# Row sums and causal convolution of the first batch on TensorE instead of DMA and GpSimd, in a fused attention, gated convolution and token-mixing kernel

## The chip, the cores and the metric

The kernel runs on one core of a Trainium2 chip. The metric is the device time of one execution in microseconds (us). TensorE (PE) multiplies and transposes, VectorE (DVE), ScalarE (ACT) and GpSimd (POOL) work elementwise, and SyncE (SP) issues all the transfers of this kernel. Each engine runs its own instructions in order and waits for the others by semaphores.

## The reference

Inputs are q, k, v of shape (4, 12, 448, 64) and seven weight matrices. Three parts follow one another:

```python
scores = where(upper triangle, -1e9, q @ k.T / 8)            # causal attention, 4 batches x 12 heads
attn = exp(scores - rowmax); attn = attn / (rowsum + 1e-9)
x = (attn @ v)                                               # (4, 448, 768)
gate_pre[s] = sum over t in 0..4 of conv_w[t] * x[s - 4 + t] # causal convolution, per channel
x = (sigmoid(gate_pre) * (x @ w_val)) @ w_out
theta = x @ w_theta
u = x + w_tok_r @ (x * cos(theta)) + w_tok_i @ (x * sin(theta))
out = u + max(u @ w_ch, 0)
```

## The kernel before

All activations lie transposed: channels on the 128 partitions, the 448 positions of a sequence along the free dimension. Heads are worked in pairs, so one pair (numbered g, 0 to 23; six to a batch) fills one block of 128 channels. A product that must be precise is split into fp32r parts: a high part, and a low part that is the rest, and three products of them are summed. Plain fp32 operands go to TensorE in the product of probabilities and v (`attn_AV`), and in all transposes.

The program is a list of attention steps, `attn_iter(i)` for each head i, with five segments each, and a list of dense steps, `dense(b)` for each batch. The attention of batch 0 and of the first heads of batch 1 is issued first, in 69 segments; then the dense steps of each batch run with the attention of the next one threaded between them. A scheduler may then move instructions within each engine's order.

A pair passes through these functions:

- `attn_T`: at the end of an odd head, q and k of the next pair are transposed, and `split_qk` copies them out of PSUM. ACT makes qs and kk, DVE makes the low parts of both; a second copy of kk is made by ACT where the table `K_DUP` has 2, and by POOL where it has 0.
- `attn_S`: scores in four chunks of 112 rows, two products each; DVE masks and takes the row maximum, ACT takes the exponential and its row sum.
- `attn_PT`: ten transposes of the probabilities, copied out of PSUM by ACT and DVE.
- `attn_R` and `attn_B`: the reciprocals of the row sums (tile rec, 112 x 8) are written to DRAM (tile rows) and read back, each row spread over 64 partitions, as the tile rb (128 x 448).
- `attn_AV`: sixteen TensorE instructions on two halves of the array, one for each head of the pair, into one PSUM tile.
- `attn_X1`: DVE multiplies that by rb into the tile xf (line 408); ACT and POOL split it into x_hi and x_lo.
- `attn_X2`: the convolution. For the first six pairs `CONV_POOL` has 1, and POOL does it: nine instructions of 128 x 448 (lines 423, 427, 430). ACT then takes tanh.
- `gemm_ahead`: six products of x_hi and x_lo with the first two column blocks of w_val, for the pairs of batch 0 alone (line 451).

Between these, DVE and ACT turn raw weights into fp32 (`to_f32`: lines 153, 156, 160 on DVE), and POOL splits the weights. The tiles in PSUM of the attention share six buffers.

The order in which a step stands comes from these lines:

```python
            if j == 1 and n == (X_LAST if g == NP else X_SEG):
                attn_X(g - 1)
```

so pair g - 1 is multiplied and convolved at the end of the odd head of pair g.

Of the kernel before, what the change touches and what calls it, by code (L numbers as in the profile page):

```python
# [14 lines left out]
ALU = mybir.AluOpType  # L15
# [6 lines left out]
ROUND = 12582912.0  # L22

X_SEG = 3
X_LAST = 3
U_DVE = (0, 1, 1, 1)
PT_DVE = (2, 2, 0, 0)
K_DUP = (2, 2, 2, 2, 2, 2, 0, 0, 0, 0, 0, 0, 0, 0, 0, 1, 0, 1, 0, 0, 0, 0, 0, 0)
X_LO = (0, 0, 0, 0, 0, 0, 0, 0, 0, 0, 0, 0, 0, 0, 1, 0, 0, 0, 0, 0, 0, 0, 0, 0)
H_LO = (1, 0, 1, 0)  # L30
O_LO = (0, 0, 0, 1)
# [18 lines left out]
def kernel(  # L50
# [49 lines left out]
    def psum(tag):  # L100
        at = "mm" if tag == "mm" else "at"
        return ps.tile([P, 512], F32, tag=at, name=f"ps_{tag}", bufs=2 if tag == "mm" else 6)
# [12 lines left out]
    def exp_set(*args, **kw):  # L115
        exps.append(nc.scalar.activation(*args, **kw))  # L116
# [131 lines left out]
    gates = {}  # L248
    rbs = {}
    row_at = {}  # L250
    ttr_ins = []
    hf_ins = []

# [115 lines left out]
    def attn_X(g):  # L369
        if not 0 <= g < B * NP:  # L370
            return
        attn_X1(g)
        attn_X2(g)

    def attn_R(g):
        if not 0 <= g < B * NP:
            return
        rec = pool.tile([CP, 2, NC], F32, tag="rec", name="rec")
        nc.vector.tensor_scalar(out=rec, in0=sums[g], scalar1=1.0e-9, scalar2=None, op0=ALU.add)
        nc.vector.reciprocal(rec, rec)  # L380
        rows = dram.tile([2, NC, CP], F32, tag="rows", name="rows", bufs=2)
        nc.sync.dma_start(out=rows.rearrange("h c p -> p h c"), in_=rec)
        row_at[g] = rows

    def attn_B(g):
        if g not in row_at:
# [30 lines left out]
    def attn_X2(g):  # L417
        b, hp = divmod(g, NP)
        x = xf[g % 2]
        gt = pool.tile([P, S], F32, tag="gate", name="gate", bufs=6)  # L420
        if CONV_POOL[g]:
            tp = pool.tile([P, S], F32, tag="tmp", name="tp")
            nc.gpsimd.tensor_scalar(
                out=gt, in0=x[:, 0:S], scalar1=cw[:, 0, hp : hp + 1], scalar2=1.0, op0=ALU.mult, op1=ALU.mult
            )
            for t in range(1, KW):
                nc.gpsimd.tensor_scalar(
                    out=tp, in0=x[:, t : t + S], scalar1=cw[:, t, hp : hp + 1], scalar2=1.0, op0=ALU.mult, op1=ALU.mult
                )
                nc.gpsimd.tensor_tensor(out=gt, in0=gt, in1=tp, op=ALU.add)  # L430
        else:
            nc.vector.tensor_scalar(out=gt, in0=x[:, 0:S], scalar1=cw[:, 0, hp : hp + 1], scalar2=None, op0=ALU.mult)
            for t in range(1, KW):
                nc.vector.scalar_tensor_tensor(  # L434
                    out=gt, in0=x[:, t : t + S], scalar=cw[:, t, hp : hp + 1], in1=gt, op0=ALU.mult, op1=ALU.add
                )
        exp_set(gt, gt, AF.Tanh, scale=0.5)
        gates[b, hp] = gt

    wn = [AHEAD]  # L440
# [172 lines left out]
    def attn_iter(i):  # L613
        g, j = divmod(i, 2)

        def seg(n):
            if j == 1 and n == (X_LAST if g == NP else X_SEG):
                attn_X(g - 1)

        attn_PT(i - 1, (0,))  # L620
        attn_S(i, 0)
# [16 lines left out]
        seg(3)  # L638
        yield
        if j == 0:  # L640
            attn_AV(g - 1)
            load_v(g + 1)
            attn_B(g - 1)
        if i == B * H:
            attn_X(g - 1)
        seg(4)
# [17 lines left out]
    for n in range(5 * (H + 1) + X_SEG + 1):  # L664
# [10 lines left out]
                        if m < AHEAD + 1:  # L675
                            split_w(m, g)
        i, c = divmod(n, 5)
        if AHEAD and i >= 4 and i % 2 == 0 and c == A_SEG and i // 2 - 2 < KC - 1:
            gemm_ahead(i // 2 - 2)
        if n == 5 * H - 3:  # L680
            with tc.issue_after(ttr_ins[-1].ins):
                for g in range(2):
                    load_w(AHEAD + 2, g)
    if AHEAD:
        gemm_ahead(KC - 1)
    for b in range(B):
        done = 0
        for y, _ in enumerate(dense(b)):
# [44 lines left out]
```

## Time and profile before

| | |
|---|---|
| median of 3 runs | 807.39 us (806.12 to 808.97) |
| profiled execution | 811.03 us, its span 809.2 us |
| TensorE busy | 725.1 us, 90% |
| VectorE, ScalarE, GpSimd busy | 493.8, 427.4, 316.2 us |
| mean granted TensorE clock | 0.949 of full speed |

The profile is of one execution. Busy time of TensorE counts an instruction from its start to its modelled end, whatever the clock; the granted clock is 1.0 at 2.4 GHz and 0.5 at 1.2 GHz. The work of the first batch's attention lies between 4 us and 124 us, where the first product of a dense step (line 472) begins. The rest of the span is dense steps with attention in between.

### The profile page before, as it was taken

What the parts mean: (1) busy time and instruction counts of PE and PEld (TensorE: products, weight loads), DVE (VectorE), ACT (ScalarE), POOL (GpSimd) and SP (SyncE); (2) the same over time, 40 slices, a digit from 0 to 9 for tenths busy, and PEclk for the clock granted to TensorE, in tenths of its full rate; (3) what the DMA queues carried; (4) which work ended last, traced back from release to release, by engine and by line L of the source; (5) the groups of instructions that cost most, each with busy time, mean ns of one, the idle gap of its engine ahead of it and who ended that gap; (6) DMA issues with size and microseconds to landing.
All of it is one profiled execution on the core that took longest, in us unless ns stands there. A gap on an engine that the chain in (4) does not pass through costs nothing.

```text
span 809.2 us, 11956 instructions
## 1 busy us (share of the span) xinstructions
PE 725.1 (90%) x3965; PEld 609.7 (75%) x3965; DVE 493.8 (61%) x1125; ACT 427.4 (53%) x998; POOL 316.2 (39%) x327
## 2 busy tenths in 40 slices
PE   5687889698598798999989899899999998999997
PEld 4455558577387686788978788788888787988996
DVE  4666869999999837535657645653666732114541
ACT  6767754465567744435687633444787622124401
POOL 0386976586355658123226610113234232201100
PEclk9888779789699999999999999999999999999999
DMA  9548627979576248778744259579824078774323
GB/s 233 125 104 182 151 47 200 236 238 294 142 221 140 63 133 225 225 234 184 157 136 86 60 144 190 148 221 196 178 58 102 12 140 215 214 212 139 98 57 90
DMA packets 151850, 126.01 MB, mean 156 GB/s; under 512 B 93519, under 2 KB 126829, under 8 KB 151789
## 3 DMA queue, kind: packets, MB, share of 16 engines
q1 hardware_dynamic: 151789, 125.25, 60.9%
q8 instruction: 31, 0.51, 0.3%
q14 instruction: 30, 0.25, 0.1%
HBM read 100.76 MB, written 24.47 MB: 155 GB/s over the span
## 4 chain that ended last, share of the span: by engine, by line
PE 54%; DVE 18%; DMA 9%; ACT 8%; POOL 6%; issue 4%; SPq 1%; ACTq 0%; POOLq 0%; DVEq 0%
PE ps_mm L472 28%; PE ps_mm L567 10%; PE ps_av L364 5%; PE ps_tr L341 3%; PE ps_s L320 2%; DVE gate L434 2%; PE ps_s L321 2%; DMA out_dram<-o 2%; DVE cv_raw L156 2%; DMA rb<-rows 2%; DMA scratch<-w_hl 2%; POOL gate L430 2%; DVE qs L111 1%; DMA rows<-rec 1%; ACT prob L116 1%
## 5 line engine op out<-in xcount | busy, mean ns | idle before, releaser
L472 PE MATMUL ps_mm<-act_hi,w_hl 128*128 128x448 f32 x864 | 274.1, 379 | 10.7 <-POOL w_hl L105 7.0
L472 PEld LDWEIGHTS ps_mm<-act_hi,w_hl 128*128 128x128 f32 x864 | 165.1, 193 | 27.9 <-POOL w_hl L105 9.4
L472 PE MATMUL ps_mm<-act_lo,w_hl 128*128 128x448 f32 x432 | 160.4, 373 | 0.0
L116 ACT ACTIVATE prob<-ps_s,negm 112x112 f32<-112x112 f32 x192 | 95.4, 498 | 71.4 <-DVE negm L322 69.4
L322 DVE CUSTOM_DVE_ANT_0 ps_s<-ps_s,mask 112x112 f32<-112x112 f32 x192 | 86.2, 454 | 76.3 <-PE ps_s L321 62.6
L320 PE MATMUL ps_s<-kk,qs 128*112 128x256 f32 x192 | 73.9, 389 | 21.3 <-DVE qs L111 4.8
L341 PE MATMUL ps_tr<-ident,prob 112*112 112x112 f32 x480 | 80.4, 271 | 13.2 <-ACT prob L116 7.6
L108 POOL TENSOR_TENSOR act_lo<-x2f,act_hi 128x448 fp32r<-128x448 f32 x36 | 43.9, 1218 | 119.8 <-ACT act_hi L486 57.0
L472 PEld LDWEIGHTS ps_mm<-act_lo,w_hl 128*128 128x128 f32 x432 | 83.4, 194 | 5.0
L354 ACT COPY pt<-ps_tr 112x448 f32<-112x448 f32 (+2 forms) x120 | 51.5, 440 | 60.7 <-PE ps_tr L341 60.2
L472 PE MATMUL ps_mm<-x_hi,w_hl 128*128 128x448 f32 x264 | 80.5, 374 | 2.3 <-ACT x_hi L413 1.1
L341 PEld LDWEIGHTS ps_tr<-ident,prob 112*112 112x112 f32 x480 | 57.3, 138 | 28.0 <-ACT prob L116 11.7
L567 PE MATMUL ps_mm<-wtok_h,zt_h 128*128 128x448 f32 x168 | 64.2, 382 | 5.6 <-ACT zt_h L558 5.6
L567 PE MATMUL ps_mm<-wtok_h,zt_l 128*128 128x448 f32 x168 | 63.6, 378 | 1.3 <-DVE zt_l L111 1.1
L321 PE MATMUL ps_s<-klo,qs 128*112 128x256 f32 x192 | 63.0, 339 | 1.4 <-DVE klo L111 1.4
L364 PE MATMUL ps_av<-pt,v_raw 112*64 112x224 f32 (+3 forms) x384 | 63.3, 446 | 0.9 <-ACT prob L116 0.8
L567 PE MATMUL ps_mm<-wtok_l,zt_h 128*128 128x448 f32 x168 | 62.3, 371 | 0.0
L320 PEld LDWEIGHTS ps_s<-kk,qs 128*112 128x112 f32 x192 | 36.6, 192 | 30.0 <-ACT kk L307 6.5
L430 POOL TENSOR_TENSOR gate<-gate,tp 128x448 f32<-128x448 f32 x48 | 57.8, 1205 | 2.8
L108 POOL TENSOR_TENSOR x_lo<-xf,x_hi 128x448 fp32r<-128x448 f32 x23 | 29.4, 1279 | 74.5 <-ACT x_hi L413 74.1
L543 POOL TENSOR_TENSOR z<-z,x2f 128x448 f32<-128x448 f32 x18 | 20.9, 1160 | 92.3 <-ACT z L540 92.3
L472 PEld LDWEIGHTS ps_mm<-x_hi,w_hl 128*128 128x128 f32 x264 | 50.3, 191 | 8.6 <-DVE hf L510 2.2
(97 smaller groups left out, 1362.0 us busy)
## 6 DMA issues: line engine op xcount, KB each, us to landing
w_hl<-scratch SPq DMA_DIRECT2D x144, 384.0 KB, 3.9
scratch<-w_hl SPq DMA_DIRECT2D x44, 384.0 KB, 4.2
q_raw<-in_q_dram SPq DMA_DIRECT2D x48, 112.0 KB, 3.6
k_raw<-in_k_dram SPq DMA_DIRECT2D x48, 112.0 KB, 3.3
v_raw<-in_v_dram SPq DMA_DIRECT2D x24, 224.0 KB, 3.9
rb<-rows SPq DMA_DIRECT2D x48, 112.0 KB, 3.9
out_dram<-o SPq DMA_DIRECT2D x24, 224.0 KB, 3.8
cv_raw<-in_moe_w_val_dram SPq DMA_DIRECT2D x12, 384.0 KB, 6.3
```

The lines of the kernel that those rows point to most:

```text
L108: nc.gpsimd.tensor_tensor(out=dst, in0=src, in1=f32(hi), op=ALU.subtract)
L116: exps.append(nc.scalar.activation(*args, **kw))
L320: nc.tensor.matmul(pt[:CP, :nn], lhsT=qs[:, cs], rhs=kk[:, :nn], start=True, stop=False)
L321: nc.tensor.matmul(pt[:CP, :nn], lhsT=qs[:, cs], rhs=klo[:, :nn], start=False, stop=True)
L322: ttr = nc.vector.tensor_tensor_reduce(out=pt[:CP, :n], in0=pt[:CP, :n], in1=mask[:, S - n : S], scale=-1.0 / math.sqrt(D), scalar=3.0e38, ...
L341: nc.tensor.transpose(pt[:CP, off : off + CP], prob[i, c][:, kc * CP : (kc + 1) * CP], ident[:CP, :CP])
L354: nc.scalar.copy(t, src)
L364: nc.tensor.matmul(av[g][j * D : (j + 1) * D, kc * CP : S], lhsT=tv[:, j, kc, :], rhs=pT.pop((2 * g + j, kc)), start=kc == 0, stop=kc == N ...
L430: nc.gpsimd.tensor_tensor(out=gt, in0=gt, in1=tp, op=ALU.add)
L472: nc.tensor.matmul(pt[:, :S], lhsT=a[:, kc % KH, :], rhs=x, start=kc == 0 and m == 0, stop=kc == KC - 1 and m == 2,)
L543: (nc.vector if Z_DVE[b] else nc.gpsimd).tensor_tensor(out=t, in0=t, in1=x2f[e], op=ALU.mult)
L567: nc.tensor.matmul(pt[:, :S], lhsT=a[:, m, :], rhs=w[:, m, :], start=m == 0 and n == 0, stop=m == NZ - 1 and n == 2,)
```

## The change

For the pairs of the first batch (g below 6) two things are done elsewhere, and the steps around them move.

- The row sums no longer go through DRAM. DVE spreads rec along the free dimension into a tile wide (112 x 512), TensorE transposes it in four pieces (`attn_W`), and ACT copies the result out of PSUM as rb.
- The convolution is five plain fp32 products on TensorE, one for each tap, with a diagonal matrix of the tap's weights as the stationary operand. POOL makes these matrices (tile dg, five of 128 x 128 for each pair) from the identity. ACT's tanh reads the PSUM tile.
- `attn_X1` of pair g - 1 comes right behind its `attn_AV`, at the end of the even head, and `attn_X2` behind the second segment of the odd head. `gemm_ahead` comes one head earlier.
- `K_DUP` is 0 for the first six pairs, so POOL makes the second copy of kk.

```diff
-K_DUP = (2, 2, 2, 2, 2, 2, 0, 0, 0, 0, 0, 0, 0, 0, 0, 1, 0, 1, 0, 0, 0, 0, 0, 0)
+K_DUP = (0, 0, 0, 0, 0, 0, 0, 0, 0, 0, 0, 0, 0, 0, 0, 1, 0, 1, 0, 0, 0, 0, 0, 0)
...
         nc.vector.reciprocal(rec, rec)
+        if g < NP:
+            wide = pool.tile([CP, NC, 2, D], F32, tag="m2k", name="wide", bufs=2)
+            nc.vector.tensor_copy(wide, rec.rearrange("p h c -> p c h").unsqueeze(3).broadcast_to((CP, NC, 2, D)))
+            wides[g] = wide
+            return
...
+    def attn_W(g):
+        wide = wides.pop(g)
+        rbs[g] = psum("tr")
+        for c in range(NC):
+            nc.tensor.transpose(
+                rbs[g][:, c * CP : (c + 1) * CP], wide[:, c].rearrange("p h d -> p (h d)"), ident[:CP, :CP]
+            )
+        rb = pool.tile([P, S], F32, tag="m2k", name="rb", bufs=2)
+        nc.scalar.copy(rb, rbs[g][:, :S])
+        rbs[g] = rb
...
-        if CONV_POOL[g]:
+        if g < NP:
+            dg = pool.tile([P, KW, P], F32, tag="z", name="dg", bufs=3)
+            for t in range(KW):
+                nc.gpsimd.tensor_scalar(
+                    out=dg[:, t, :], in0=ident, scalar1=cw[:, t, hp : hp + 1], scalar2=1.0, op0=ALU.mult, op1=ALU.mult
+                )
+            src = psum("tr")
+            for t in range(KW):
+                nc.tensor.matmul(src[:, :S], lhsT=dg[:, t, :], rhs=x[:, t : t + S], start=t == 0, stop=t == KW - 1)
+            src = src[:, :S]
+        elif CONV_POOL[g]:
...
-        exp_set(gt, gt, AF.Tanh, scale=0.5)
+        exp_set(gt, src, AF.Tanh, scale=0.5)
...
-            if j == 1 and n == (X_LAST if g == NP else X_SEG):
+            if j == 1 and g > NP and n == X_SEG:
                 attn_X(g - 1)
+            if j == 1 and 1 <= g <= NP and n == 1:
+                attn_X2(g - 1)
...
         if j == 0:
+            if g - 1 in wides:
+                attn_W(g - 1)
             attn_AV(g - 1)
             load_v(g + 1)
             attn_B(g - 1)
+            if 1 <= g <= NP:
+                attn_X1(g - 1)
...
-        if AHEAD and i >= 4 and i % 2 == 0 and c == A_SEG and i // 2 - 2 < KC - 1:
-            gemm_ahead(i // 2 - 2)
+        if AHEAD and i >= 3 and i % 2 == 1 and c == A_SEG:
+            gemm_ahead((i - 3) // 2)
...
-    if AHEAD:
-        gemm_ahead(KC - 1)
```

TensorE, at the passage from an odd head to the next pair. Before, the transposes of q and k (q_raw, k_raw) follow the last score chunk (klo_75 is of odd heads, klo_74 of even ones), and the probabilities of the odd head and the new pair's scores come at once:

```order
L321 MATMUL ps_s<-klo_75,qs 112x448
L283 MATMUL ps_tr<-ident,q_raw 128x112 x4
L283 MATMUL ps_tr<-ident,k_raw 128x112 x4
L341 MATMUL ps_tr<-ident,prob 112x112 x4
L320 MATMUL ps_s<-kk,qs 112x256
```

In the changed kernel, from the middle of the odd head on:

```order
L445 MATMUL ps_tr<-xf_72,dg 128x448 x5
L341 MATMUL ps_tr<-ident,prob 112x112 x3
L479 MATMUL ps_mm<-x_hi,w_ahead 128x448 x2
L320 MATMUL ps_s<-kk,qs 112x336
L321 MATMUL ps_s<-klo_75,qs 112x336
L320 MATMUL ps_s<-kk,qs 112x448
L321 MATMUL ps_s<-klo_75,qs 112x448
L283 MATMUL ps_tr<-ident,q_raw 128x112 x4
L479 MATMUL ps_mm<-x_lo,w_ahead 128x448
L479 MATMUL ps_mm<-x_hi,w_ahead 128x448
L283 MATMUL ps_tr<-ident,k_raw 128x112 x4
```

The five convolution products stand between the second and the third score chunk, and four of the six products of `gemm_ahead` now stand between the transposes of q and of k (the two rows shown come twice there).

VectorE, at the same passage. Before, xf stands between the two instructions on rec, ahead of the low parts of k (klo_74) and of the next scores:

```order
L111 TENSOR_TENSOR qs<-ps_tr,qs 64x448
L379 TENSOR_SCALAR rec<-sums 112x8
L408 TENSOR_TENSOR xf_73<-ps_av,rb 128x448
L380 RECIPROCAL rec<-rec 112x8
L111 TENSOR_TENSOR klo_74<-ps_tr,kk 64x448
```

In the changed kernel wide has its place there, and xf stands ahead of the first chunk of the next odd head:

```order
L110 TENSOR_TENSOR klo_74<-ps_tr,kk 64x448
L383 COPY wide<-rec 112x512
L110 TENSOR_TENSOR qs<-ps_tr,qs 64x448
L110 TENSOR_TENSOR klo_75<-ps_tr,kk 64x448
...
L159 SCALAR_TENSOR_TENSOR cv_raw<-cv_raw 128x384
L424 TENSOR_TENSOR xf_72<-ps_av,rb 128x448
L322 ISA ps_s,negm<-ps_s,mask 112x112
```

So xf moved from the passage between two pairs to the place behind `attn_AV`.

TensorE, where the dense steps begin. Before, `attn_AV` of the next batch's first pair and the first scores of another head stand ahead of the first dense product (w_hl):

```order
L364 MATMUL ps_av<-pt,v_raw 64x336 x2
L364 MATMUL ps_av<-pt,v_raw 64x224
L451 MATMUL ps_mm<-x_lo,w_ahead 128x448
L451 MATMUL ps_mm<-x_hi,w_ahead 128x448
...
L341 MATMUL ps_tr<-ident,prob 112x112 x2
L320 MATMUL ps_s<-kk,qs 112x256
L321 MATMUL ps_s<-klo_75,qs 112x256
L341 MATMUL ps_tr<-ident,prob 112x112 x2
L472 MATMUL ps_mm<-x_hi,w_hl 128x448
```

In the changed kernel:

```order
L283 MATMUL ps_tr<-ident,q_raw 128x112 x4
L479 MATMUL ps_mm<-x_lo,w_ahead 128x448
L479 MATMUL ps_mm<-x_hi,w_ahead 128x448
...
L283 MATMUL ps_tr<-ident,k_raw 128x112 x4
L341 MATMUL ps_tr<-ident,prob 112x112 x3
L500 MATMUL ps_mm<-x_hi,w_hl 128x448
```

The scores of one even head, its `attn_AV` and two chunks of the next head moved behind the beginning of the dense steps.

## Rows read from the trace of the kernel before

**Rows 1.** The page, engines: busy us, share of the span, instructions.
```profile
PE 725.1 (90%) x3965; PEld 609.7 (75%) x3965; DVE 493.8 (61%) x1125; ACT 427.4 (53%) x998; POOL 316.2 (39%) x327
```
**Rows 2.** Stretches between `attn_AV`s: length, PE, PEld, DVE, ACT, POOL, clock, DMA.
```profile
23.08:39.89 16.81, 11.31 (x62) 7.86 (x62) 10.25 (x32) 11.91 (x35) 7.12 (x9) 0.85 0.49 112
39.89:54.46 14.57, 12.51 (x67) 8.10 (x66) 10.62 (x30) 10.61 (x29) 10.73 (x13) 0.85 0.42 103
54.46:72.05 17.59, 15.31 (x71) 10.63 (x70) 12.63 (x32) 11.87 (x34) 15.15 (x17) 0.69 0.68 117
72.05:87.21 15.16, 11.28 (x64) 7.82 (x63) 11.44 (x35) 11.99 (x33) 9.51 (x11) 0.84 0.99 237
87.21:101.75 14.54, 12.68 (x67) 8.14 (x66) 11.44 (x34) 11.05 (x32) 13.66 (x15) 0.85 0.47 117
...
101.75:109.20 7.45, 7.33 (x47) 5.00 (x46) 5.92 (x13) 3.50 (x11) 6.08 (x7) 0.92 0.16 35
109.20:121.47 12.27, 9.01 (x36) 5.57 (x35) 6.27 (x20) 7.24 (x21) 8.65 (x11) 0.72 0.28 55
...
121.47:180.00 58.53, 50.13 (x243) 40.96 (x242) 56.80 (x105) 29.28 (x66) 39.21 (x35) 0.85 0.83 222
180.00:280.00 100.00, 79.54 (x424) 65.63 (x424) 91.78 (x184) 65.39 (x144) 54.26 (x57) 0.91 0.65 180
```
**Rows 3.** Line 408 (xf) up to 150 us: what it waits for, who waits.
```profile
  DMA rb<-rows: 8.1, 5
  PE ps_s L320: 4.1, 3
```
**Rows 4.** TensorE timeline, fifth passage: start, length, waits in brackets.
```profile
87.21 1.02 PE L364 MATMUL ps_av<-pt,v_raw 112*64 112x448 f32 x2
...
95.15 0.59 PE L341 MATMUL ps_tr<-ident,prob 112*112 112x112 f32 x3
96.89 0.31 PE L341 MATMUL ps_tr<-ident,prob 112*112 112x112 f32 x1 [1.16 <-ACT prob L116]
97.56 0.38 PE L320 MATMUL ps_s<-kk,qs 128*112 128x256 f32 x1 [0.36 <-POOL kk L105]
...
99.47 0.58 PE L320 MATMUL ps_s<-kk,qs 128*112 128x336 f32 x1 [0.34 <-DVE qs L111]
...
101.75 2.68 PE L364 MATMUL ps_av<-pt,v_raw 112*64 112x448 f32 x14
```
**Rows 5.** TensorE timeline, the plain fp32 products of line 364 in four short windows.
```profile
23.08 2.10 PE L364 MATMUL ps_av<-pt,v_raw 112*64 112x448 f32 x14 [0.84 <-ACT prob L116]
...
54.47 4.00 PE L364 MATMUL ps_av<-pt,v_raw 112*64 112x448 f32 x14
...
291.07 0.60 PE L364 MATMUL ps_av<-pt,v_raw 112*64 112x448 f32 x2
...
291.07 0.97 PE L364 MATMUL ps_av<-pt,v_raw 112*64 112x448 f32 x4
```
**Rows 6.** Groups of POOL, 15 to 124 us: busy us, mean ns.
```profile
L430 POOL TENSOR_TENSOR gate<-gate,tp 128x448 f32<-128x448 f32 x24 | 28.7, 1198 | 1.6
L427 POOL TENSOR_SCALAR tp<-xf,cw 128x448 f32<-128x448 f32 x24 | 17.5, 729 | 0.9
L423 POOL TENSOR_SCALAR gate<-xf,cw 128x448 f32<-128x448 f32 x6 | 4.8, 805 | 15.0 <-DVE rec L380 9.1 <-DVE xf L408 5.9
```
**Rows 7.** DVE and POOL timelines, one conversion with POOL idle and one behind line 108.
```profile
24.59 0.36 DVE L153 TENSOR_SCALAR cv_raw<-cv_raw 128x384 int32<-128x384 uint32 x1
...
67.39 1.17 DVE L153 TENSOR_SCALAR cv_raw<-cv_raw 128x384 int32<-128x384 uint32 x1
...
67.20 1.14 POOL L108 TENSOR_TENSOR x_lo<-xf,x_hi 128x448 fp32r<-128x448 f32 x1
```
**Rows 8.** DVE timeline, the last xf of the batch and the first dense step.
```profile
111.48 0.62 DVE L408 TENSOR_TENSOR xf<-ps_av,rb 128x448 f32<-128x448 f32 x1 [2.07 <-DMA rb<-rows]
...
121.47 0.62 DVE L510 SCALAR_TENSOR_TENSOR hf<-gate,ps_mm 128x448 f32<-128x448 f32 x1 [2.92 <-PE ps_mm L451]
```

More of the change, by code (lines that the diff above doesn't have):

```diff
@@ L24 @@
 X_SEG = 3
-X_LAST = 3
 U_DVE = (0, 1, 1, 1)
 PT_DVE = (2, 2, 0, 0)
-K_DUP = (2, 2, 2, 2, 2, 2, 0, 0, 0, 0, 0, 0, 0, 0, 0, 1, 0, 1, 0, 0, 0, 0, 0, 0)
+K_DUP = (0, 0, 0, 0, 0, 0, 0, 0, 0, 0, 0, 0, 0, 0, 0, 1, 0, 1, 0, 0, 0, 0, 0, 0)
 X_LO = (0, 0, 0, 0, 0, 0, 0, 0, 0, 0, 0, 0, 0, 0, 1, 0, 0, 0, 0, 0, 0, 0, 0, 0)
@@ L250 @@
     row_at = {}
+    wides = {}
     ttr_ins = []
@@ L420, in attn_X2 @@
         gt = pool.tile([P, S], F32, tag="gate", name="gate", bufs=6)
-        if CONV_POOL[g]:
+        if g < NP:
[9 more added lines that the diff above has]
+        elif CONV_POOL[g]:
+            src = gt
             tp = pool.tile([P, S], F32, tag="tmp", name="tp")
@@ L431, in attn_X2 @@
         else:
+            src = gt
             nc.vector.tensor_scalar(out=gt, in0=x[:, 0:S], scalar1=cw[:, 0, hp : hp + 1], scalar2=None, op0=ALU.mult)
```

## The prediction

> **What bounds the kernel now.** I read the page's line of engines first [rows 1]: TensorE is busy for 725.1 of 809.2 us, so in the long run anything put on it costs time, unless it stands where TensorE waits or runs slowly. The change touches only the attention of the first batch, so the next view is the stretches [rows 2], cut at the starts of `attn_AV`, one for each pair. There TensorE is neither full nor fast. The five stretches from 23.08 to 101.75 us take 78.7 us, 15.7 each. In the last and least disturbed of them (14.54 us) TensorE is busy for 12.68 us and idle for 1.86. Its granted clock is 0.85 there, between the levels of 2.4 GHz (1.0) and 1.2 GHz (0.5), so the 12.68 us hold about 12.68 x 0.85 = 10.8 us of full-speed work, and the low level costs about 1.9. Room per pair is thus 1.9 + 1.9 = 3.8 us in this stretch, and more in the first and third.
>
> What TensorE waits for stands in two groups. DVE waits 8.1 us in five of the xf for rb to come back from DRAM, and TensorE waits 4.1 us behind that [rows 3]. Where rb is hardly late, the passage from one pair to the next still has gaps: 1.16 us for the last exponential, 0.36 us for kk, 0.34 us for a low part [rows 4].
>
> From 121.47 to 280 us another engine has the say: DVE is busy for 56.80 of 58.53 us and then for 91.78 of 100 [rows 2]. Whatever DVE work is pushed behind 121.47 is paid there.
>
> **What it removes.** The wait for rb goes: DVE's 8.1 us and TensorE's 4.1 with it [rows 3]. POOL's convolution goes: 28.7 + 17.5 + 4.8 = 51.0 us [rows 6]. POOL was not what the stretches waited for, so I put nothing in the sum for its own time. Its side effect is on DVE: a conversion takes 0.36 us when POOL does nothing, and 1.17 us (67.39 to 68.56) when it starts behind a POOL instruction that runs from 67.20 to 68.34 [rows 7]. The Trainium skill has a rule for this (SBUF — State Buffer, Who interferes with whom): VectorE and GpSimd share one pair of SBUF ports as an exclusive lock, and the second to come is blocked until the first ends. The trace agrees; by that rule alone most of these long conversions would become short ones, which speaks for the faster rival below. Since I build the new stretch from the fifth one, in which they are few, the sum has no further term for them.
>
> **What it adds.** *Convolution.* No plain fp32 product of 128 x 128 by 128 x 448 stands in the trace; the nearest is `attn_AV`. Its products of 448 columns appear as two records each, for two halves of the array that start together: two records in the first 0.4 us, four in 0.97 [rows 5]. So 448 columns take two slots of about 0.375 us: (0.97 - 0.60) is the step from the first two to the next. A product that fills the array then costs 2 x 0.375 = 0.75 us, five cost 3.75. If instead the halves ran behind one another, the sixteen records of one `attn_AV`, 2240 columns like the five taps, would price the five at the 2.1 us of the fourteen seen at 23.08 plus one pair of records, some 2.3. At the low clock the same fourteen take 4.00 [rows 5], so 3.75 would be some 7.5. I take 3.75, because the records start in pairs.
> *Spreading.* Four transposes of 112 columns: a block of three takes 0.59 us with its tail [rows 4], so some 0.45 of TensorE's order; none if they fit a gap. The copy wide has 512 elements on DVE: between nothing, in its gaps, and the 0.62 us of xf [rows 8]; rec is ready a whole head before the transposes want wide, so I hide it. ACT's copy of rb lies beside `attn_AV`, which needs 2.1 us anyway [rows 5]; uncovered it would be about the same 0.6.
> *POOL.* Thirty small dg and twelve copies of kk: at most 0.73 us each [rows 6], 31 us in place of 51, hidden while POOL is free. The copy of kk that ACT made is now in POOL's queue behind dg; it was so in the fifth passage (0.36 us of waiting, [rows 4]), so that is in my base.
> *xf.* Behind `attn_AV` in DVE's order, xf holds up the next head's row maxima. Those scores come later on TensorE than `attn_AV` too, so up to 0.6 us per pair would show only if DVE is late.
>
> **The sum.** A pair: 10.8 of work at full clock + 3.75 + 0.45 = 15.0, plus gaps. The fifth stretch has 1.86 us of gaps; four products of `gemm_ahead`, some 0.8 us, now stand between the transposes of q and k and fill part of them, so 1.1 remain: 16.1. Let s be what the low clock costs per pair. Before, s was 1.9 in the best stretch; I take 0.4, because a block of 3.75 us of products without a wait now stands in every pair ahead of the passage, and the gaps are shorter. So 16.5 against 15.7 before. The first `attn_AV` comes at 23.08 + 0.45 = 23.5, the sixth at 23.5 + 5 x 16.5 = 106.0 instead of 101.75: 4.3 late.
>
> Then something is won. Before, 19.7 us lie between the sixth `attn_AV` and the first dense step on DVE (hf, 121.47): a wait of 2.07 for rb, a clock of 0.72, and a head of the next batch that stands first [rows 2, 8]. After, the way is the 7.45 us to 109.20, of which 7.33 x 0.92 = 6.7 at full clock, plus 3.75 and two products (0.4): 10.9. So hf comes at 116.9, which is 4.6 us early. But the next batch's head is then still to be done. Its part of DVE is 6.27 less the xf of 0.62, or 5.65 us, and it lands where DVE has 58.53 - 56.80 = 1.7 us free: 4.0 to 5.6 are paid back. Net: -4.6 + 5.4 = **+0.8 us**. The profiled execution took 811.03 us for a span of 809.2, 0.45% above the median of 807.39; the same step from the median gives **808 us**, no change that this kernel's measurement can tell (0.3%, or 2.4 us).
>
> **The rivals.**
> *Faster: TensorE is kept full.* With DVE never behind POOL and no wait for rb, DVE and ACT catch up during the 3.75 us, the gaps fall to 0.3 and the clock stays at 2.4 GHz: a pair takes 15.3, five save 6.0 on my sum, 802 us. (The lower price for the five products takes 1.4 per pair off, 7 in all: 801 from my sum, 795 from this case; since the records start in pairs I let the range end at 801.) For it: DVE and ACT have only 10 to 12.6 us of work per stretch [rows 2]. Against it: the 1.16 us gap is a chain of score, maximum and exponential that no free engine shortens.
> *Slower: the clock still falls in each passage.* The place is the passage, whose gaps of 1.16, 0.36 and 0.34 are none of rb's; in that stretch the clock was 0.85 although rb was hardly late. If s stays near 2, five pairs cost 8 more: 816 us. It decides from s = 0.7 on, where the sum passes +2.4. The Trainium skill has the mechanism (TensorE: Matmul & The Clock Gate, HAM oscillation — how this bites in real kernels): gaps between bursts of products throttle the clock anew each time. The trace agrees in that every stretch before has a mean clock of 0.69 to 0.85.
> *The change does not do what it says: one wait takes the place of the other.* xf no longer waits for DRAM but for `attn_AV` and rb's copy, and DVE stands with all row maxima behind it. At 0.6 us per pair, 3 us: 811.
>
> **Chances and range.** No change 0.36 (808), TensorE kept full 0.32 (802), clock falls in each pair 0.20 (816), wait exchanged 0.12 (811). Faster 0.32, within 0.3% 0.36, slower 0.20 + 0.12 = 0.32. Both signs hold most of the chance, so the range reaches to both ends, 801 to 816; of the likeliest case alone it would be 805 to 810.
>
> **What would show it.** In the profile after: ten records at the convolution's line for each pair of heads, two for a tap, 3.7 to 3.9 us from the first to the last at full clock (2.3 would speak for the lower price); no wait of DVE for a transfer before the first dense step; stretches between `attn_AV`s of 16 to 17 us; a granted clock over 0.9 in them; hf near 117; and DVE as full as before up to 280 us. I would be wrong by the first term if the stretches come out at 15.3 or less, by s if the clock in them is still 0.85 or lower with the low level costing about 2 us, and by the give-back if hf comes early and the rest of the kernel is not longer.

## The result, and the profile after

The changed kernel takes **819.16 us** (median of 4 runs, 818.56 to 821.06); the kernel before took 808.18 beside it (4 runs, 806.12 to 812.58). The ratio is 1.0133, 95% interval 1.0087 to 1.0179: some 11 us slower. I had forecast 808, no change, with a range of 801 to 816. The profiled execution took 819.33 us for a span of 817.5; against the 809.2 of [rows 1] that is 8.3 us, because the execution profiled before lay above its own median.

The engines' line of the page after, which answers to [rows 1]:

```profile
PE 733.6 (90%) x4049; PEld 616.6 (75%) x4049; DVE 490.5 (60%) x1131; ACT 422.8 (52%) x992; POOL 282.3 (35%) x315
```

The stretches after, cut at the starts of `attn_AV` or up to 0.34 us ahead of them, at the first hf (117.07) and at the eleventh `attn_AV` (301.90), from which on TensorE is busy for 95% of the time (columns as in [rows 2]):

```profile
22.96:39.43 16.47, 13.90 (x81) 9.62 (x80) 10.73 (x33) 10.89 (x32) 7.49 (x12) 1.00 0.33 92
39.43:54.46 15.03, 13.62 (x81) 9.64 (x80) 9.71 (x34) 10.50 (x32) 7.24 (x12) 1.00 0.32 86
54.46:69.08 14.62, 13.19 (x81) 9.36 (x80) 9.27 (x31) 10.37 (x32) 5.88 (x11) 1.00 0.40 115
69.08:91.26 22.18, 16.46 (x81) 11.15 (x80) 15.63 (x48) 13.59 (x41) 5.86 (x7) 0.83 0.66 175
91.26:107.56 16.30, 14.44 (x82) 9.71 (x80) 9.40 (x29) 9.75 (x28) 4.00 (x5) 0.92 0.41 116
107.56:117.07 9.51, 9.51 (x56) 6.37 (x55) 3.73 (x15) 5.48 (x20) 1.14 (x1) 1.00 0.23 63
...
117.07:301.90 184.83, 146.57 (x757) 119.28 (x755) 160.00 (x317) 104.71 (x239) 99.22 (x99) 0.90 0.62 171
301.90:817.50 515.60, 491.39 (x2776) 430.17 (x2775) 259.28 (x592) 245.02 (x546) 142.53 (x143) 0.99 0.60 151
```

The kernel before, in the two stretches that answer to the last two:

```profile
121.47:291.07 169.60, 140.75 (x726) 116.49 (x724) 154.03 (x302) 99.22 (x222) 100.87 (x99) 0.90 0.67 183
...
291.07:809.20 518.13, 491.55 (x2776) 430.04 (x2775) 258.96 (x592) 244.96 (x546) 143.05 (x143) 0.99 0.59 150
```

Add it up. To the first `attn_AV` nothing changes (23.08, now 22.96). The five pairs take 84.6 us in place of 78.7: +5.9. From the sixth `attn_AV` to the first hf it is 9.5 in place of 19.7: -10.2. From hf to the eleventh `attn_AV` it is 184.8 in place of 169.6: **+15.2**. The rest is 2.5 shorter. So hf comes at 117.07, as forecast (116.9), and what is lost is lost in two places: one pair of the five, and the dense part behind hf.

*The fourth pair.* Three of the first four pairs take 16.5, 15.0 and 14.6 us at a clock of 1.00; the fourth takes 22.18. DVE's timeline there:

```profile
73.40 0.14 DVE L322 DVE_READ_ACCUMULATOR2_ANT negm<- 112x1 f32 x1
78.17 0.36 DVE L152 TENSOR_SCALAR cv_raw<-cv_raw 128x384 int32<-128x384 uint32 x1 [4.62 <-DMA cv_raw<-in_moe_w_val_dram]
```

DVE stands for 4.62 us on the conversion of a weight tile that has not landed (and once more, for 3.74 us, in the fifth pair). Row maxima are queued behind it, exponentials wait for those, and TensorE waits in turn. TensorE's timeline of the passage that follows:

```profile
81.87 0.31 PE L341 MATMUL ps_tr<-ident,prob 112*112 112x112 f32 x1 [1.27 <-ACT prob L115]
83.76 0.43 PE L341 MATMUL ps_tr<-ident,prob 112*112 112x112 f32 x1 [1.58 <-ACT prob L115]
...
90.50 0.98 PE L394 MATMUL ps_tr<-ident,wide 112*128 112x112 f32 x4 [2.58 <-DVE wide L383]
```

From 83.6 to 93.8 us the granted clock is 0.5: the only low stretch between 20 and 117 us. Why the tile is late stands in SyncE's queue:

```profile
65.02 0.85 SPq L261 DMA_DIRECT2D k_raw<-in_k_dram  x2
72.12 0.31 SPq L269 DMA_DIRECT2D v_raw<-in_v_dram  x1
72.56 2.69 SPq L194 DMA_DIRECT2D cv_raw<-in_moe_w_val_dram  x3
```

The load of v waits until `attn_AV` has given up v's buffer (72.1), and three weight loads stand behind it in the queue. Before the change the order was the other way round:

```profile
66.87 2.10 SPq L195 DMA_DIRECT2D cv_raw<-in_moe_w_val_dram  x4
75.35 0.33 SPq L269 DMA_DIRECT2D v_raw<-in_v_dram  x1
```

*Behind hf.* DVE's work there grew from 154.03 to 160.00 us, by the displaced head, as forecast. But its idle time grew as well, from 15.6 to 24.8 us; 6.3 us of it are waits for w_out, of which there were none before. The first of them, on DVE's timeline:

```profile
128.03 0.61 DVE L110 TENSOR_TENSOR act_lo<-hf,act_hi 128x448 fp32r<-128x448 f32 x1
131.32 0.36 DVE L152 TENSOR_SCALAR cv_raw<-cv_raw 128x384 int32<-128x384 uint32 x1 [2.68 <-DMA cv_raw<-in_moe_w_out_dram]
131.71 0.28 DVE L322 CUSTOM_DVE_ANT_0 ps_s<-ps_s,mask 112x112 f32<-112x112 f32 x1
...
134.86 0.36 DVE L152 TENSOR_SCALAR cv_raw<-cv_raw 128x384 int32<-128x384 uint32 x1 [1.98 <-DMA cv_raw<-in_moe_w_out_dram]
```

Again DVE waits for weight tiles, now of w_out, and again row maxima stand behind: those of head 14, which come 17 us later than before the change (131.71; 114.97 before).

*The products* cost what the higher of my two prices said, that of records that start in pairs. TensorE's timeline, four transposes of wide and one convolution:

```profile
68.63 0.55 PE L394 MATMUL ps_tr<-ident,wide 112*128 112x112 f32 x4
...
73.08 3.94 PE L445 MATMUL ps_tr<-xf,dg 128*128 128x448 f32 x10
```

Ten records in pairs, 3.94 us from the first start to the last end; I had 3.75, and 0.45 for the transposes.

### The profile page after: what moved, and what is told of

Its sections match the earlier page's. It is cut to its first block, busy times and chain, and to the rows that moved or that the text cites. A ratio compares the mean times of both kernels' runs of the same rounds, so it can differ in the third digit from the quotient of the medians.

```text
span 817.5 us, 12108 instructions
## 1 busy us (share of the span) xinstructions
PE 733.6 (90%) x4049; PEld 616.6 (75%) x4049; DVE 490.5 (60%) x1131; ACT 422.8 (52%) x992; POOL 282.3 (35%) x315
## 4 chain that ended last, share of the span: by engine, by line
PE 50%; DVE 23%; DMA 12%; ACT 7%; issue 4%; POOL 2%; SPq 1%; ACTq 0%; DVEq 0%; POOLq 0%
PE ps_mm L500 25%; PE ps_mm L595 10%; DMA out_dram<-o 4%; PE ps_av L364 4%; PE ps_tr L341 3%; DVE cv_raw L159 2%; DVE gate L462 2%; DVE cv_raw L155 2%; DMA cv_raw<-in_moe_w_out_dram 2%; DVE ps_s L322 2%; DVE qs L110 2%; PE ps_tr L445 2%; PE ps_s L320 2%; DVE cv_raw L152 2%; PE ps_s L321 2%
## 5 line engine op out<-in xcount | busy, mean ns | idle before, releaser
L500 PEld LDWEIGHTS ps_mm<-act_hi,w_hl 128*128 128x128 f32 x864 | 163.2, 191 | 22.4 <-POOL w_hl L104 3.5
L320 PE MATMUL ps_s<-kk,qs 128*112 128x256 f32 x192 | 70.6, 372 | 14.7 <-POOL kk L104 7.0
L595 PE MATMUL ps_mm<-wtok_h,zt_h 128*128 128x448 f32 x168 | 64.7, 385 | 2.8 <-ACT zt_h L586 2.8
L321 PE MATMUL ps_s<-klo,qs 128*112 128x256 f32 x192 | 60.1, 327 | 1.3 <-DVE klo L110 1.2
L364 PE MATMUL ps_av<-pt,v_raw 112*64 112x448 f32 (+3 forms) x384 | 58.4, 430 | 3.2 <-DVE pt L352 2.6
L104 POOL TENSOR_SCALAR w_hl<-cv_raw 128x384 fp32r<-128x384 f32 x44 | 31.3, 713 | 67.8 <-DVE cv_raw L159 30.0
L364 PEld LDWEIGHTS ps_av<-pt,v_raw 112*64 112x64 f32 x384 | 27.9, 143 | 33.7 <-issue 18.5
```

Source lines behind the costliest of these rows:

```text
L104: nc.gpsimd.tensor_scalar(out=dst, in0=src, scalar1=1.0, scalar2=0.0, op0=ALU.mult, op1=ALU.add)
L320: nc.tensor.matmul(pt[:CP, :nn], lhsT=qs[:, cs], rhs=kk[:, :nn], start=True, stop=False)
L321: nc.tensor.matmul(pt[:CP, :nn], lhsT=qs[:, cs], rhs=klo[:, :nn], start=False, stop=True)
L364: nc.tensor.matmul(av[g][j * D : (j + 1) * D, kc * CP : S], lhsT=tv[:, j, kc, :], rhs=pT.pop((2 * g + j, kc)), start=kc == 0, stop=kc == N ...
L500: nc.tensor.matmul(pt[:, :S], lhsT=a[:, kc % KH, :], rhs=x, start=kc == 0 and m == 0, stop=kc == KC - 1 and m == 2,)
L595: nc.tensor.matmul(pt[:, :S], lhsT=a[:, m, :], rhs=w[:, m, :], start=m == 0 and n == 0, stop=m == NZ - 1 and n == 2,)
```

## The experiments

Each ratio is to the kernel before, timed beside the other; where two kernels are set against one another I take the difference of their ratios times 809 us.

**The two parts apart.** One kernel takes the spreading alone into the kernel before:

```diff
+        if g < NP:
+            wide = ...
+            wides[g] = wide
+            return
...
+            if g - 1 in wides:
+                attn_W(g - 1)
             attn_AV(g - 1)
```

> The kernel before, with one part of the change: reciprocal row sums spread by four transposes and ACT's copy; the convolution stays on GpSimd and every other step where it was. Theory (the products, not the spreading, lengthen a pair): DVE's 8.1 us of waits for rb go and with them TensorE's 4.1, a pair costs 0.45 more of transposes; hf near 119 and 804 to 808 in all. Rival (hf early is given back by DVE's work behind it, as in the changed kernel): 808 to 815.

Measured: 800.0 us (797.54 to 802.63), ratio 0.9881 (0.9852 to 0.9911). Faster than I expected, and faster than both kernels. Its stretches, first to last pair and from hf on:

```profile
23.60:37.30 13.70, 11.96 (x72) 8.80 (x71) 11.69 (x35) 12.08 (x34) 9.96 (x12) 0.88 0.40 111
...
83.70:100.90 17.20, 13.85 (x73) 10.11 (x72) 15.75 (x41) 12.02 (x35) 13.75 (x16) 0.80 0.31 86
115.30:282.40 167.10, 141.55 (x720) 116.47 (x718) 153.50 (x302) 102.89 (x224) 103.61 (x101) 0.92 0.70 186
```

hf comes 6.2 us early and the eleventh `attn_AV` 8.7: nothing is given back. Another takes the convolution alone (the new branch of `attn_X2`, where GpSimd's stood):

> The kernel before, with the other part alone: the convolution as five products on TensorE, in the place where GpSimd's stood; rb still comes through DRAM. Theory (3.9 us of products per pair are hidden only as far as TensorE stood idle): pairs of 16.5 to 18 us, the sixth attn_AV 4 to 10 us later than 101.75, 812 to 820. Rival (they fill the wait for rb and raise the clock): sixth attn_AV at 102 or earlier, 805 to 810.

Measured: 819.25 us (815.29 to 820.53), ratio 1.0113 (1.0083 to 1.0142). The pairs take 16.9 to 21.3 us, the sixth `attn_AV` starts at 117.5, hf at 133.4. The first reading holds, beyond its bound. What TensorE waits for in the five pairs, most of all:

```profile
PE ps_tr L429 <- DVE xf L408: 11.6, 4, 5.3
```

The products stand in TensorE's order behind an xf that waits for rb, and all scores stand behind the products. They don't fill the wait; they carry it over to TensorE. And the changed kernel with GpSimd's convolution back in `attn_X2`, everything else as changed:

> The changed kernel with the convolution on GpSimd again (spreading by transposes and the new places of xf, gates and gemm_ahead stay). It takes the 3.9 us of five products out of each pair. If the products stand on the path in full (one tap instead of five gave 3.0 us per pair): stretches of 11 to 13 us, hf near 97 to 100, total 790 to 800. Rival (GpSimd's 51 us slow DVE's conversions and x_lo comes late, so that the products were worth their place): 802 or more.

Measured: 799.97 us (799.36 to 801.42), ratio 0.9885 (0.986 to 0.991), within the first reading in time, but not by its stretches:

```profile
22.80:99.50 76.70, 63.18 (x351) 45.63 (x351) 65.98 (x170) 54.31 (x159) 65.21 (x75) 0.83 0.45 126
107.90:281.50 173.60, 143.63 (x750) 119.78 (x748) 156.34 (x316) 106.73 (x238) 112.17 (x104) 0.91 0.67 181
```

The first three pairs take 15.3, 14.7 and 14.2 us here, 14.7 on average against 15.4 with the products. So in an undisturbed pair the products are nearly paid for by what GpSimd's convolution costs; most of the loss lies elsewhere.

**The late load of the fourth pair.** The loads of v for pairs 3 to 6 go to GpSimd's queue, so that no weight load stands behind them:

```diff
-        v_ins[g] = nc.sync.dma_start(
+        v_ins[g] = (nc.gpsimd if 2 < g < 7 else nc.sync).dma_start(
```

> The changed kernel, with the loads of v for pairs 3 to 6 issued from GpSimd's queue instead of SyncE's, so that no weight load stands behind a load that waits for attn_AV. Theory A (a late weight load is the fault in the fourth stretch): the three cv_raw loads are issued near 66 us instead of 72.6, DVE's wait of 4.62 us goes, the fourth stretch falls from 22.2 us to about 15, no low clock at 83.6, hf near 110 instead of 117.1. If the rest is as long as in the changed kernel, 819.2 - 7 = 812. Rival B (the weight and attention work on DVE after the first dense step sets the end, so an earlier hf is given back): stretch and hf as above, but 817 to 821 in all. Rival C (the wait is not from the queue but from the DVE itself): the fourth stretch stays over 20 us.

Measured: 811.96 us (809.79 to 815.45), ratio 1.0044 (1.0023 to 1.0066): 7.2 us less than the changed kernel, theory A's 812. SyncE's queue and the fourth stretch:

```profile
64.34 0.85 SPq L261 DMA_DIRECT2D k_raw<-in_k_dram  x2
65.28 2.04 SPq L194 DMA_DIRECT2D cv_raw<-in_moe_w_val_dram  x4
```
```profile
68.60:86.20 17.60, 15.24 (x80) 10.54 (x80) 15.06 (x43) 12.35 (x35) 7.00 (x8) 0.90 0.64 194
```

The weight loads leave at 65.28, DVE's wait of 4.62 is gone, and the stretch is 17.6 us, not the 15 I named: DVE still has 15 us of work in it, and the clock still falls there (0.90). hf comes at 112.96. A second edit, meant for something else, shows the same: the second copy of kk goes back to ACT.

```diff
-K_DUP = (0, 0, 0, 0, 0, 0, 0, ...
+K_DUP = (2, 2, 2, 2, 2, 2, 0, ...
```

> The changed kernel with the second copy of kk on ACT again for the first six pairs (the table K_DUP as before). If the kk on GpSimd, which stands there in order and waits for ACT, holds up the passage: each pair 0.3 to 0.6 us shorter, 814 to 817. If it is hidden (my working had it in the base): the first three stretches within 0.3 us of 16.5, 15.0 and 14.6.

Measured: 813.55 us (811.26 to 819.53), ratio 1.0059 (1.0037 to 1.0082). Neither reading: the first three stretches are longer by 2 us together (15.7, 16.4 and 16.0), yet the kernel is 6 us faster. In SyncE's queue the weight loads now stand ahead of v's:

```profile
67.25 0.85 SPq L261 DMA_DIRECT2D k_raw<-in_k_dram  x2
68.20 1.50 SPq L194 DMA_DIRECT2D cv_raw<-in_moe_w_val_dram  x3
75.10 0.33 SPq L269 DMA_DIRECT2D v_raw<-in_v_dram  x1
```

and the fourth stretch is 17.5 us. The kernels that have the whole change and five products agree: in the six in which v's load stands ahead of the weight loads the fourth stretch takes 22.0 to 22.4 us, in the four in which it does not 17.5 to 17.6. So the order of these loads decides 5 us, and it turns over with small edits elsewhere.

**The dense part.** The diagonal matrices take the three buffers in which the token weights are loaded; given buffers of x2f instead:

```diff
-            dg = pool.tile([P, KW, P], F32, tag="z", name="dg", bufs=3)
+            dgs = [pool.tile([P, 3, P], F32, tag="x2f", name="dg", bufs=6) for _ in range(2)]
+            dg = [dgs[t // 3][:, t % 3, :] for t in range(KW)]
```

> The changed kernel, with the diagonal matrices in buffers of x2f (idle until 150 us) instead of the three buffers of z, in which the token weights are loaded. Theory A: the first three tok_bits loads are issued near 12 us as before the change, SyncE no longer stands at 77, 99 and 114 us until a convolution is done; the loads of w_out behind them come earlier, and DVE's waits for cv_raw between 128 and 135 us (2.68 and 1.98) shrink. Worth up to 4.7 us: 814 to 817. The fourth stretch stays at 22 us, since its loads stand behind v's. Rival B (DVE's own work sets the pace there): 817 to 821.

Measured: 811.9 us (810.78 to 815.09), ratio 1.0043 (1.0023 to 1.0062). A gain of 7.3 us, more than theory A allowed, and not by its mechanism: DVE's waits for w_out are still 4.9 us, hf still comes at 117.5. The gain lies later, where the conversions are stretched less: DVE is busy for 152.84 us in place of 160.00 from hf to the eleventh `attn_AV`, with the same 317 instructions, and the 96 conversions among them take 58.3 us in place of 64.7. With v's loads moved as well:

> Both edits of the two runs before: v's loads of pairs 3 to 6 from GpSimd's queue, diagonal matrices out of z's buffers. Theory A: the sum of the two gains, 806 to 811, about the kernel before the change. Rival B: hf near 110 but 817 to 821.

Measured: 810.61 us (807.77 to 817.46), ratio 1.0029 (1.0003 to 1.0054). That is inside theory A's 806 to 811, but only 1 us better than either edit alone: the two gains don't add. Token loads moved out of the first w_out loads (`TOK_LOAD` from 3, 5, 7, 9 to 7, 9, 10, 11):

> The changed kernel with the token weights loaded some steps later (table TOK_LOAD), so that two of their loads no longer stand among the first loads of w_out. If the bunched transfers make w_out late: DVE's waits for w_out up to the sixth hf fall from 4.7 to under 2 us, head 14's maxima come up to 4 us earlier, 812 to 816. If not: the waits stay at 4 to 5 us and 817 to 821.

Measured: 820.91 us (817.96 to 823.74), ratio 1.0141 (1.0105 to 1.0177), and the waits are 6.3 us: the token loads among them are not the cause. The next two try to bring the next batch's head ahead of hf again, the first by putting the last products of `gemm_ahead` behind the loop:

```diff
-        if AHEAD and i >= 3 and i % 2 == 1 and c == A_SEG:
+        if AHEAD and i >= 3 and i % 2 == 1 and c == A_SEG and i < 13:
...
+    gemm_ahead(KC - 1)
```

> The changed kernel, with the last pair's products of gemm_ahead put behind the whole loop again, so that the next batch's head stands ahead of the dense steps as before the change. Give-back as I forecast it (the head's 5.65 us of DVE work are only moved): hf 4 to 6 us later, the dense part shorter by as much, total within 2 us of the changed kernel, 817 to 821. If the early start is itself the fault (the dense steps outrun the loads of their weights and the head's scores come 17 to 22 us late): 810 to 815.

Measured: 811.69 us (808.99 to 813.79), ratio 1.0036 (1.0018 to 1.0053), a time within the second reading. The second edit writes six more attention steps ahead of the dense steps:

> The changed kernel, with six more steps of attention written ahead of the dense steps (and six fewer called for behind them), so that head 14's scores and the seventh attn_AV stand ahead of the first dense step, as they did in the trace before. Theory D (the displaced head is the fault: its row maxima stand in DVE's order behind conversions whose loads have not landed, so that it comes 17 to 22 us late): hf 5 to 9 us later, DVE's 5 us of waits for w_out before 136 us gone, from hf to the eleventh attn_AV 168 to 173 us instead of 184.9, total 809 to 813. Rival (dense part long for another reason): from hf to the eleventh attn_AV 178 us or more, total 819 to 824.

Measured: 814.71 us (812.28 to 817.15), ratio 1.0056 (1.0035 to 1.0078). It lies between the two readings. In both, 56 row maxima still stand ahead of the first hf on DVE, as in the changed kernel (60 before): the order was not restored, and neither tells what it was made for. Yet both are faster, and from hf to the eleventh `attn_AV` they take 174.1 us and

```profile
117.40:294.70 177.30, 149.91 (x758) 123.17 (x757) 155.96 (x317) 108.74 (x241) 103.14 (x99) 0.89 0.67 178
```

An ordering edge, added to the second, restores the order:

```diff
+            with ExitStack() as st:
+                if b == 0 and e == 0:
+                    st.enter_context(tc.issue_after(ttr_ins[-1].ins))
                 hf_ins.append(
```

> As the run with the head first, and hf of the first dense step held by an ordering edge behind head 14's last row maximum, so that the head does stand ahead of it on DVE (60 row maxima before the first hf instead of 56, as before the change). Theory D (the head pushed behind the dense start costs more than its 5.65 us of DVE work, because its maxima queue behind conversions that wait for loads of w_out): DVE's waits for w_out up to the sixth hf fall from 5 us to under 2, from hf to the eleventh attn_AV 166 to 171 us (167 to 170 in the three kernels that had the head ahead, 174 to 185 in those that had not), total 806 to 812. Rival (where the head stands does not matter): hf later by 4 to 6 us and a total of 814 to 822.

Measured: 812.54 us (805.85 to 816.68), ratio 1.0024 (0.9999 to 1.0049): 8.8 us less than the changed kernel. The dense part, and what DVE waits for until 148 us:

```profile
125.50:294.30 168.80, 139.93 (x727) 115.57 (x724) 152.69 (x304) 102.14 (x227) 97.07 (x97) 0.92 0.66 184
```
```profile
DVE cv_raw L152 <- DMA cv_raw<-in_moe_w_out_dram: 1.0, 1, 1.0
```

168.8 us, inside theory D's 166 to 171, though hf comes 8.4 later; the wait is 1.0 in place of 4.7, and the total lies just above theory D's 806 to 812. But the stretch is shorter in part because hf, where it begins, comes later. The six steps alone gave 6.2 of the 8.8 us; the edge adds 2.6, and the two intervals overlap. Counted from the sixth `attn_AV` to the eleventh, the changed kernel takes 194.3 us (189.3 before), this one 184.0, and three kernels in which the head still stands behind hf take 183.9 (last products of `gemm_ahead` late), 185.2 (buffers of x2f) and 186.7 (six steps alone). So these runs do not show that the place of the head is what cost the time. With v's loads moved as well:

> The same with v's loads of pairs 3 to 6 on GpSimd's queue. If the two faults are apart from one another (late weight load in the fourth stretch 5 to 7 us, displaced head), their gains add: total 801 to 807, about the kernel before or better. If they are one fault seen twice: as the better of the two, 809 to 812.

Measured: 807.11 us (803.48 to 812.08), ratio 0.9979 (0.9957 to 1.0002). 12.5 us less than the changed kernel; one by one the edits gave 7.2 and 8.8, and over the move of v's loads alone (1.0044) the held hf gives 5.3, clear of the noise. So each gives something that the other does not, and together they take the changed kernel back to the time of the kernel before:

```profile
24.50:104.50 80.00, 69.76 (x401) 47.91 (x401) 54.71 (x162) 54.13 (x156) 34.55 (x50) 0.99 0.46 128
122.40:290.80 168.40, 139.03 (x729) 113.76 (x725) 152.68 (x304) 102.15 (x227) 96.44 (x97) 0.93 0.68 184
```

**The price of a product.** First the changed kernel with one tap in place of five (four are left out of the sums):

```diff
-            for t in range(KW):
+            for t in (KW - 1,):
```

> The changed kernel with one product per convolution in place of five (four taps are left out of the sums, so the output differs). It frees about 3 us of TensorE per pair, 18 in all. If the products' price stands on the path: the sixth attn_AV 10 to 15 us earlier, hf near 102 to 105. Theory B (what the first batch gains is given back): total still 812 or more. Rival (a us gained in the first batch is kept): 801 to 806.

Measured: 791.55 us (790.04 to 794.49), ratio 0.978 (0.9753 to 0.9807), below every reading. hf comes at 97.6. The first three stretches:

```profile
23.30:36.10 12.80, 11.47 (x73) 8.24 (x72) 9.73 (x28) 9.56 (x29) 7.49 (x12) 0.94 0.43 118
36.10:48.90 12.80, 10.79 (x72) 8.03 (x72) 10.21 (x34) 10.36 (x32) 7.38 (x12) 1.00 0.37 101
48.90:60.50 11.60, 10.21 (x72) 7.84 (x72) 9.12 (x30) 10.13 (x30) 5.90 (x11) 1.00 0.52 146
```

They are 8.9 us shorter for 12 products, or 0.74 each, and the time is kept: theory B, that what the first batch gains is given back, is refuted. The kernel gains 28.6 us, more than 24 products at 0.74 (18), because more than the products goes: though v's load still stands ahead of three weight loads, DVE waits only 0.6 us for them, the fourth stretch takes 15.2 us in place of 22.2, and from hf to the eleventh `attn_AV` it is 177.3 in place of 184.8. Then with hf held and v's loads moved (the two mends, as they are called below), one tap, and ten (the five done twice):

> The run with hf held and v's loads on GpSimd's queue (807.1), with one product per convolution in place of five (four taps are left out of the sums, so the output differs). If each product stands on the path in full (0.75 us at the full clock): 24 products, 18 us, 787 to 791. If they fill time in which TensorE would stand idle or run at the low clock: 798 or more.

> The same with the five products done twice over (the convolution's sums are doubled, so the output differs). If each product stands on the path in full: 30 more, 22.5 us, 827 to 832. If half is hidden: 815 to 822.

Measured: 790.57 (789.24 to 797.25), ratio 0.9758 (0.9736 to 0.978), and 832.97 (829.77 to 835.56), ratio 1.0284 (1.0258 to 1.031). Against 0.9979 in the middle, 24 products fewer save 17.9 us, 0.75 each, and 30 more cost 24.7, 0.82 each. By the time of the whole kernel each product stands on the path in full. The stretches of five pairs in the two kernels, one tap first:

```profile
23.80:92.10 68.30, 59.49 (x361) 42.21 (x360) 54.88 (x160) 52.80 (x154) 34.92 (x50) 0.92 0.52 150
```
```profile
24.20:122.70 98.50, 89.69 (x453) 58.21 (x452) 56.43 (x162) 54.83 (x155) 33.83 (x50) 0.98 0.36 104
```

Beside the 80.0 us with five taps these are 11.7 less for twenty products, 0.59 each, and 18.5 more for twenty-five, 0.74 each. The one-tap execution is the slowest of its six, 0.8% above their median, and its clock is 0.92.

Last, GpSimd's convolution under the same two mends, and with v's loads moved alone:

> The same with the convolution on GpSimd again. If the remaining 7 us between 807.1 and the 800.0 of the kernels without the products are the products' net price, and the two faults arise only with the products: 797 to 802, as without the mending. If the mending is worth something here too: 790 to 796, and the products' net price is 11 to 17 us.

> The changed kernel with the convolution on GpSimd again, and v's loads of pairs 3 to 6 on GpSimd's queue. Its fourth stretch is 16.9 us with v on SyncE: if a late load is in it, 1.5 to 2 us less, 797 to 799; if v's loads hold up GpSimd, which has the convolution to do, 801 to 806.

Measured: 810.23 us (804.38 to 811.79), ratio 0.9995 (0.9976 to 1.0014), and 808.85 (804.76 to 811.83), ratio 0.9986 (0.9959 to 1.0012). Neither reading of the first held: the mend costs some 9 us. The second, slower than either of its readings, shows that nearly all of it is v's loads: with these on GpSimd's queue the five pairs take 84.3 us in place of 76.7, and holding hf as well changes 0.1%. GpSimd, which has the convolution to do, waits 1.8 us for `attn_AV` there and spends 3.6 us on the four loads; how 7.6 us come of this is not shown. So the move of v's loads helped the kernels whose GpSimd was free of the convolution, and cost time in those where it was not.

## Why the prediction was wrong, point by point

- **The pair's sum** came out at 16.5 us; the first three stretches took 15.4 on average. The five products (3.94, I had 3.75) and the transposes (0.55, I had 0.45) were right, and so was the higher of the two prices. The base was too high: without them the 13.2 to 13.9 us of TensorE leave about 9.1, not 10.8, for the same number of records (81 less 14). The gaps came to 1.8 us a pair, not 1.1; most of those in the first three pairs are waits for GpSimd's copy of kk, 3.3 us in all. As to the base, busy time counts a record that stands alone in full, some 0.36 us, where records in a row start 0.2 us apart, so that work full of waits looks longer than it is; I think this is the reason, and have not tested it. And s was 0, not 0.4: the clock was 1.00. The rival "TensorE is kept full" had the clock right and its 15.3 nearly so, but by luck: it had the gaps fall to 0.3, with the same base. The other rival needed the clock to fall in each of these passages; it did not in the first three, in spite of waits of up to 1.4 us. The case that the Trainium skill tells of (TensorE: Matmul & The Clock Gate, HAM oscillation — how this bites in real kernels) is one in which the wait between two bursts of products is longer than the burst. Here the waits are far shorter than the work between them, so the section does not say that the clock falls here, and I leaned on it too far.
- **What was missing in the pairs**: DVE's wait of 4.62 us in the fourth, for a weight tile whose load stands behind v's in SyncE's queue. I had counted the removed transfers (rows, rb) but not looked at the order of that queue after the change. Their going alone does not turn it over: they are gone too in the changed kernel with GpSimd's convolution and in the one with kk on ACT, and there the weight loads stand first. 5.7 us too little here and 3.4 too much in the first three nearly cancel: the sixth `attn_AV` came at 107.56, forecast 106.0. That is luck. With v's loads moved, 7.2 us came back.
- **The passage to hf** was right in its way, and 1.4 us too long: 9.5 us, forecast 10.9. That hf came at 117.07, forecast 116.9, is luck again, since the sixth `attn_AV` was 1.6 late.
- **The give-back is the step that failed.** I put 5.4 us, a value between the displaced head's work on DVE less its free time (4.0) and all of it (5.6). The stretch behind hf was 15.2 us longer. The work was right (154.03 to 160.00), but no free time was used: DVE's idle time grew by 9.3, and waits for loads of w_out, for which my sum had nothing, are 6.3 us of its idle time. Behind the earlier hf the conversions of w_out stand where their loads have not landed, and the head's maxima wait behind them. Whether the place of the head brought the loss stays open: holding hf until the head is done took the stretch from 184.8 to 168.8, but from the sixth `attn_AV` to the eleventh three kernels that did not restore the order gained about as much (183.9 to 186.7 in place of 194.3; 184.0 with hf held).
- **The rivals.** "The clock falls in each passage" (816) is nearest in time and false in its cause: behind the waits of 1.27 and 1.58 us it fell once, and not in each pair. "One wait takes the place of the other" had its own wait about right (xf waited for `attn_AV` 3.5 us in all, forecast 3), but TensorE waited for xf only once, for 1.4 us; the costly waits were for weights.
- **GpSimd's convolution was not free**, as I had it. Six single products less would bring the one-tap kernel with both mends from 0.9758 to about 0.970; the two kernels with GpSimd's convolution and rb by transposes stand at 0.988. The difference, 1.8% or some 14 us, is what GpSimd's convolution costs here, worked out from kernels that differ in more than the convolution, and not measured by itself. The thirty products cost some 22.4, so the exchange loses 8 us (0.9979 against 0.9881): in the profiled executions of the run with both mends and of the spreading alone, whose spans differ by 6.1 us, it is 2.7 in the five pairs, 3.5 between the sixth `attn_AV` and hf, where the sixth convolution stands, 1.3 from hf to the eleventh `attn_AV`, 0.9 ahead of the first, and 2.3 less at the end.
- **What of that is conversions.** Between 20 us and hf the thirty-six steps of converting weight tiles on DVE took 24.1 us before and 18.7 after. DVE's groups before:

```profile
L160 DVE SCALAR_TENSOR_TENSOR cv_raw<-cv_raw 128x384 int32<-128x384 int32 x12 | 8.6, 726 | 2.0 <-ACT cv_raw L159 2.0
L156 DVE SCALAR_TENSOR_TENSOR cv_raw<-cv_raw 128x384 int32<-128x384 int32 x12 | 8.5, 713 | 0.2
L153 DVE TENSOR_SCALAR cv_raw<-cv_raw 128x384 int32<-128x384 uint32 x12 | 7.0, 588 | 1.0 <-DMA cv_raw<-in_moe_w_val_dram 1.0
```

and after:

```profile
L159 DVE SCALAR_TENSOR_TENSOR cv_raw<-cv_raw 128x384 int32<-128x384 int32 x12 | 7.4, 617 | 3.5 <-ACT cv_raw L158 3.4
L155 DVE SCALAR_TENSOR_TENSOR cv_raw<-cv_raw 128x384 int32<-128x384 int32 x12 | 6.7, 556 | 0.1
L152 DVE TENSOR_SCALAR cv_raw<-cv_raw 128x384 int32<-128x384 uint32 x12 | 4.6, 385 | 8.8 <-DMA cv_raw<-in_moe_w_val_dram 8.8
```

The rule of the Trainium skill that I weighed (SBUF — State Buffer, Who interferes with whom) says that GpSimd and VectorE lock one another out of the pair of SBUF ports that they share; these 5.4 us agree with it. The last row shows the other side too: what DVE won in work it lost in waiting for loads, 8.8 us in place of 1.0.

**What stays open.** Among the kernels in which the head is displaced, the stretch from hf to the eleventh `attn_AV` ranges from 173.6 to 185.9 us, and small edits (buffers, a table) move it by up to 11. With hf held it is 168.4 to 174.5, which meets that range. Part is DVE's idle time, part the stretching of its conversions, but which edit brings which I can't say; so what made the changed kernel's dense part one of the longest is not shown. Why the first w_out loads land late is not settled either; the token loads are not it.

## What to carry to other kernels

When a change moves steps, read the order of the loads in their queue again: a load that must wait for its buffer can come to stand ahead of loads that others need, and here that cost 5 us of one stretch. Price an engine swap by both ends: the products cost their full 0.75 us each, and GpSimd's convolution, which nothing seemed to wait for, cost, as worked out above, some two thirds as much through others. And time the parts of a change alone: the spreading by itself gives 1.2%, and is the version to keep.

## What was not expected of the hardware

The granted clock was 1.00 over stretches in which TensorE was idle for 1.4 to 2.6 of 14.6 to 16.5 us; in the run with the spreading alone it was 0.79 to 0.88 over stretches of much the same length, with 1.7 to 3.4 us idle. So the clock did stay up, which I gave too small a chance, and that did not make the kernel faster. My reason for it, a block of 3.75 us of products without a wait in every pair, is not what the runs show: with one product in place of five the clock of the first three stretches was still 0.94, 1.00 and 1.00, and with GpSimd's convolution in the same order of steps 0.81, 0.85 and 0.88. What keeps it up is not shown.
